# Memory-augmented recurrent attention, forward and backward: the segment chain carries 8 memory tokens instead of 40 tokens

## The chip, the cores and the metric

One core of one Trainium2 chip runs the whole program. The metric is the device time of one execution in microseconds (us), the median of several runs. The profile is one further execution under the hardware profiler; the times of single instructions come from it.

## The reference

Two attention layers over the same 2,048 tokens of 576 features are mixed by a gate, and all gradients are asked for besides the output. Layer A is multi-query attention with 32 heads of 18 (one shared key and value head). Layer B is the recurrent one, and the change touches it alone:

```python
# H = 32 heads of Dh = 128, M = 8 memory tokens, seg_len = 32, n_seg = 64
mask = (idx[:, None] < M) | (idx[:, None] >= idx[None, :])
mem = mem0
for s in range(n_seg):
    xs = x[:, s * seg_len:(s + 1) * seg_len, :].copy()
    h = jnp.concatenate([mem, xs], axis=1)
    q = jnp.einsum('btd,dhe->bhte', h, Wq)      # k and v alike
    scores = jnp.einsum('bhqe,bhke->bhqk', q, k) * scale
    p = _softmax(jnp.where(mask[None, None], scores, -1000000000.0), axis=-1)
    o = jnp.einsum('bhqk,bhke->bhqe', p, v)
    o = jnp.einsum('bhte,hed->btd', o, Wo)
    mem = o[:, :M, :].copy()
    outs.append(o[:, M:, :])
out = g * a + (1 - g) * concatenate(outs)       # g = sigmoid(sum(x * gate_w))
```

Only the 8 memory rows of a segment's output go into the next segment. They are queries over the 32 tokens and the 8 old memory tokens. The 32 token rows are queries too, but what they give is read by nobody within the loop. The kernel returns the output and the gradients of x, of A's four weights, of mem0, of Wq, Wk, Wv, Wo and of the gate's weights.

## The kernel before, in words

Matrices are bf16, sums fp32 in PSUM. A framework takes the program of each engine from the Python loops, allocates tiles from pools with a number of buffers each (`bufs`), sets all semaphores, and orders every engine's instructions ahead of time; an instruction may stand earlier than the loops have it where its operands and buffers allow (the weights of layer B are loaded during pass 2 of layer A). On the chip each engine then works through its list in order. DMAs are issued by SyncE (SP) and GpSimd (POOL), each in its own order too.

`build_full` (L1096) runs these stages one after the other, each with pools of its own:

- **Part A** (`prep`, `a_weights`, `a_setup`, `a_pass1`, `a_pass2`, `a_out`, L717 to L1006): layer A's attention. It also stores x and the weighted gradient of the output, transposed, in DRAM (`xT_dram`, `dbT_dram`). Its pass 2 contains groups of four matmuls on four column strips of TensorE (L984).
- **Forward chain** (`b_forward`, L219): a loop over the 64 segments. `hTs` holds the segment's 32 tokens and 8 memory tokens, transposed and padded to 64 columns. For each of q, k, v, 200 matmuls (L252) make the [64 tokens x 4,096] product in two column halves, with 102 or 103 moving columns each (`pieces`), four banks being evicted by VectorE and ScalarE in turn (`evac`, L88). The 32 heads are transposed on TensorE (L268), scored with the mask added by a second matmul (L282, L284), exponentiated (L287), summed by a matmul with ones (L291), and inverted as a 64x512 reciprocal, four times (L293). Two products give the attention output transposed (L304) and by token (`km_to_tm2`, L307), and 192 matmuls of 8 columns with `WoN` (L314, L317) give the next memory, which L321 to L326 copy into the next `hTs`. q, k, v, the probabilities and outputs of every segment go to DRAM (`st_*`, `ox_dram`, `om_dram`).
- **Weight transposes** (`make_transposed_weights`, L190): all four weights, 640 transposes, through two PSUM buffers, to `st_WT` and `st_WoT`.
- **Combine** (`combine_pass`, L639): per 128 tokens the output product with `WoN` on four column strips (L665), the gate's mix, the output and the gate's gradient.
- **Backward chain** (`b_backward`, L398): the transposed weights are loaded, then the 64 segments run from the last to the first: the output gradient of 40 tokens through `WoT` (L425), score gradients (L448 to L453), the gradients of q, k, v both transposed (L469, L481, L501) and by token (`km_to_tm2`), and 480 matmuls of 40 columns (L515) that give the gradient of the segment's input. Its 8 memory rows are the start of the earlier segment (`gTs`, L523), its 32 token rows go to `dxB_dram`.
- **Weight gradients** (`b_epilogue`, L539): per 512 columns, 20 tiles of 128 tokens (16 of x, 4 of memory) against the gradients of q, k, v (2,400 matmuls), then per 128 columns the same for Wo (1,280 matmuls), with loads of 128x128 pieces (L626).
- **Part A's end** (`a_final`, L1024).

Of the kernel before, what the change touches and what calls it, by code (L numbers as in the profile page):

```python
# [6 lines left out]
ACT = mybir.ActivationFunctionType  # L7
# [13 lines left out]
LP = 64  # L21
# [8 lines left out]

MNK_LIMIT = 960000
BIG_LIMIT = None


def plane(h):
    return h // 16


def ucol(h):
    return (h % 16) // 4, (h % 4) * 128  # L40


def pieces(N, M, K, limit="default"):
    lim = MNK_LIMIT if limit == "default" else limit
    if lim is None or M * N * K <= lim:
        return [(0, N)]
    maxn = max(1, lim // (M * K))
    n = (N + maxn - 1) // maxn
    base = N // n
    rem = N % n  # L50
    out = []
    lo = 0
    for i in range(n):
        sz = base + (1 if i < rem else 0)
        out.append((lo, lo + sz))
        lo += sz
    return out


def pieces_b(N, M, K):  # L60
    return pieces(N, M, K, limit=BIG_LIMIT)


class Kern:
# [41 lines left out]
    def setup_consts(self, pool):  # L106
# [7 lines left out]
        self.onesB = pool.tile([P, 64], BF16, name="onesB")  # L114
        nc.gpsimd.memset(self.onesB[:], 1.0)
        self.negonesB = pool.tile([P, 64], BF16, name="negonesB")
        nc.gpsimd.memset(self.negonesB[:], -1.0)
        mb = pool.tile([P, 64], BF16, name="maskbias")
        nc.gpsimd.memset(mb[:], 0.0)
        nc.gpsimd.affine_select(out=mb[0:64], in_=mb[0:64], compare_op=ALU.is_ge, fill=NEGB,  # L120
                                base=0, pattern=[[1, 64]], channel_multiplier=-1)
        nc.gpsimd.affine_select(out=mb[0:64], in_=mb[0:64], compare_op=ALU.is_ge, fill=0.0,
                                base=31, pattern=[[0, 64]], channel_multiplier=-1)
        nc.gpsimd.affine_select(out=mb[0:64], in_=mb[0:64], compare_op=ALU.is_ge, fill=NEGB,
                                base=39, pattern=[[0, 64]], channel_multiplier=-1)
        nc.gpsimd.affine_select(out=mb[0:32], in_=mb[0:32], compare_op=ALU.is_ge, fill=NEGB,
                                base=39, pattern=[[-1, 64]], channel_multiplier=0)
        nc.gpsimd.affine_select(out=mb[32:64], in_=mb[32:64], compare_op=ALU.is_ge, fill=0.0,
                                base=39, pattern=[[-1, 64]], channel_multiplier=0)
        nc.gpsimd.affine_select(out=mb[32:40], in_=mb[32:40], compare_op=ALU.is_ge, fill=NEGB,  # L130
                                base=39, pattern=[[-1, 64]], channel_multiplier=0)
        self.maskbias = mb

    def setup_dram(self, dram):
        T, NSEG, NM = self.T, self.NSEG, self.NM
        NMP = ((NM + P - 1) // P) * P
        self.xT_dram = dram.tile([NKT, P, T], BF16, name="xT_dram")
        self.st_q2 = dram.tile([NSEG, P, 2048], BF16, name="st_q2")
        self.st_k2 = dram.tile([NSEG, P, 2048], BF16, name="st_k2")
        self.st_vT = dram.tile([NSEG, P, 2048], BF16, name="st_vT")  # L140
        self.st_pnT = dram.tile([NSEG, P, 2048], BF16, name="st_pnT")
        self.st_oT = dram.tile([NSEG, P, 2048], BF16, name="st_oT")
        self.st_WT = dram.tile([3, HB, P, D], BF16, name="st_WT")
        self.st_WoT = dram.tile([NKT, P, J], BF16, name="st_WoT")
        self.ox_dram = dram.tile([T, J], BF16, name="ox_dram")
        self.om_dram = dram.tile([NMP, J], BF16, name="om_dram")
# [1068 lines left out]
```

## Time and profile before

| | us |
|---|---|
| three runs | 13,498.41, 13,510.95, 13,515.17 |
| median | 13,510.95 |
| the profiled execution | 13,530.5 |
| its span, first to last instruction | 13,528.8 |
| PE (TensorE matmul) busy | 11,751.1 (87%) |
| VectorE (DVE) busy | 5,404.0 (40%) |
| ScalarE (ACT) busy | 4,011.9 (30%) |
| GpSimd (POOL) busy | 1,399.6 (10%) |
| mean granted TensorE clock | 0.655 of full speed |
| DMA | 788.49 MB, mean 58 GB/s |

In the lines of the profile L252 and its like appear as L99 and L104: these are the helpers `mm` and `tr` that issue every matmul and transpose, so groups are told apart by their tiles (`pbank<-Wv,hTs` is the projection of v into the PSUM tile `pbank`). "PEld" is the loading of weights into TensorE, which overlaps with matmuls. A group's line gives busy time, then the mean duration of one in ns, then the idle time of the engine before it and what ended it. A timeline's line gives start, duration from the first start to the last end, and, after x, how many instructions were merged. Durations of matmuls overlap, so their rate is read from the starts.

### The profile page before, as it was taken

How to read it: one execution, taken by the hardware profiler on the slowest of the kernel's cores; microseconds unless marked ns; L12 is line 12 of the kernel's file. 1: busy time of each engine (PE TensorE's matmuls, PEld its weight loads, DVE VectorE, ACT ScalarE, POOL GpSimd, SP SyncE). 2: the span in 40 equal slices, each digit the busy share in tenths (PEclk: the TensorE clock that was granted, in tenths of full speed). 3: DMA queues.
4: the chain of work that ended last, by engine and by line, in shares of the span. 5: the costliest groups of instructions: out<-in, count | busy, mean ns of one | idle time of the engine just before them, and what ended most of it. 6: DMA issues, size and time to landing. Idle time of an engine off the chain costs nothing. (4 is left out here: it accounts for less than half of the span.)

```text
span 13528.8 us, 358100 instructions
## 1 busy us (share of the span) xinstructions
PE 11751.1 (87%) x163974; PEld 7294.4 (54%) x163974; DVE 5404.0 (40%) x5901; ACT 4011.9 (30%) x7182; POOL 1399.6 (10%) x2859
## 2 busy tenths in 40 slices
PE   6777777999999999998999999975999999999887
PEld 2222221111266666666666666654878887787333
DVE  5666667888633333333333333321333333333000
ACT  4666666777511111111111111110222222222000
POOL 1111111000000000000000000011111101100235
PEclk9888886555555555555555555556777777767998
DMA  1000003111111111111111111134222222222434
GB/s 56 9 9 9 9 9 96 48 48 48 62 40 37 39 38 38 38 38 37 41 37 39 37 39 37 39 131 144 79 79 82 80 77 79 79 74 76 145 119 110
DMA packets 438733, 788.49 MB, mean 58 GB/s; under 512 B 190529, under 2 KB 279314, under 8 KB 434338
## 3 DMA queue, kind: packets, MB, share of 16 engines
q1 hardware_dynamic: 328930, 458.23, 10.7%
q0 software_dynamic: 108288, 307.35, 6.9%
q8 instruction: 1281, 20.99, 0.6%
q14 instruction: 234, 1.92, 0.0%
HBM read 431.16 MB, written 334.17 MB: 57 GB/s over the span
## 5 line engine op out<-in xcount | busy, mean ns | idle before, releaser
L99 PEld LDWEIGHTS <-hTs 128*64 128x64 bf16 (+1 forms) x38400 | 1854.6, 150 | 886.9 <-ACT hTs L322 25.7
L892 DVE TENSOR_TENSOR a_W<-a_dP,a_E 128x1024 bf16<-128x1024 f32 x1024 | 1251.5, 1224 | 572.8 <-ACT a_E L891 480.3
L979 DVE TENSOR_TENSOR b_dS<-b_dP,b_E 128x1024 bf16<-128x1024 f32 x1024 | 1235.6, 1223 | 204.6 <-PE b_S L99 153.9
L891 ACT ACTIVATE a_E<-a_S 128x512 bf16<-128x512 f32 x2048 | 1115.9, 596 | 447.2 <-PE a_S L99 388.1
L978 ACT ACTIVATE b_E<-b_S 128x512 bf16<-128x512 f32 x2048 | 1110.9, 595 | 349.1 <-DVE b_dS L979 183.2
L293 DVE RECIPROCAL rden<-pbank 64x512 f32<-64x512 f32 x256 | 849.3, 3338 | 424.8 <-PE pbank L99 420.7
L99 PE MATMUL b_S<-b_KV,b_QD 32*128 32x512 bf16 x2048 | 888.1, 583 | 32.0 <-DMA b_QD<-qd_dram 31.9
L99 PE MATMUL pbank<-Wv,hTs 128*64 128x103 bf16 (+3 forms) x12800 | 912.4, 290 | 0.0
L99 PE MATMUL a_acc<-a_W,a_WK 128*64 128x512 bf16 x2048 | 473.0, 449 | 383.6 <-DVE a_W L892 383.4
L99 PE MATMUL pbank<-Wqk,hTs 64*64 64x102 bf16 (+1 forms) x5120 | 752.7, 290 | 0.0
L99 PE MATMUL pbank<-WoT,gTs 128*64 128x103 bf16 (+3 forms) x12800 | 694.9, 239 | 56.5 <-DMA WoT<-st_WoT 56.2
L99 PE MATMUL pbank<-Wq,hTs 128*64 128x103 bf16 (+1 forms) x10240 | 710.1, 290 | 21.6 <-ACT hTs L322 20.3
L99 PE MATMUL pbank<-Wk,hTs 128*64 128x103 bf16 (+1 forms) x10240 | 711.0, 290 | 0.0
L99 PE MATMUL b_acc<-b_dS,b_SD 128*32 128x512 bf16 x2048 | 619.6, 601 | 12.2 <-DVE b_dS L979 10.2
L99 PEld LDWEIGHTS <-gTs 128*64 128x64 bf16 (+1 forms) x12800 | 488.9, 120 | 257.1 <-issue 57.1
L99 PE MATMUL b_acc<-b_E,b_SD 128*32 128x512 bf16 x2048 | 620.3, 602 | 3.1 <-DMA b_SD<-sd_dram 2.1
L99 PE MATMUL b_dP<-b_KV,b_QD 32*128 32x512 bf16 x2048 | 615.1, 597 | 0.0
L99 PE MATMUL a_S<-a_QD,a_KV 32*128 32x512 bf16 x2048 | 539.4, 441 | 45.6 <-ACT a_QD L866 43.1
L99 PEld LDWEIGHTS <-a_WK 128*64 128x64 bf16 x2048 | 193.9, 111 | 688.1 <-issue 681.6
L99 PE MATMUL a_acc<-a_E,a_VK 128*64 128x512 bf16 x2048 | 521.3, 443 | 31.2 <-ACT a_E L891 26.9
L99 PE MATMUL pkq<-maskbias,identB 64*64 64x64 bf16 x2048 | 532.5, 260 | 0.0
L99 PE MATMUL pkq<-qT,kT 128*64 128x64 bf16 x2048 | 532.3, 260 | 0.0
(349 smaller groups left out, 16671.6 us busy)
## 6 DMA issues: line engine op xcount, KB each, us to landing
b_SD<-sd_dram SPq DMA_DIRECT2D x64, 512.0 KB
b_QD<-qd_dram SPq DMA_DIRECT2D x64, 512.0 KB
st_q<-q SPq DMA_DIRECT2D x64, 512.0 KB
st_k<-k POOLq DMA_DIRECT2D x64, 512.0 KB, 3.0
st_vT<-vT SPq DMA_DIRECT2D x64, 512.0 KB
st_pnT<-pnT SPq DMA_DIRECT2D x64, 512.0 KB
st_oT<-oT POOLq DMA_DIRECT2D x64, 512.0 KB, 3.1
bq<-st_q SPq DMA_DIRECT2D x64, 512.0 KB
```

Source lines behind the costliest of these rows:

```text
L99: return self.nc.tensor.matmul(out, lhsT, rhs, start=start, stop=stop, tile_position=tp, skip_group_check=True)
L293: nc.vector.reciprocal(rden[rows, :], den[rows, :])
L891: nc.scalar.activation(Et[:, i, :], S[i][:, :], ACT.Exp, scale=SCALEA)
L892: nc.vector.tensor_tensor(out=Wt[:], in0=dP[:], in1=Et[:], op=ALU.mult)
L978: nc.scalar.activation(Et[:, i, :], S[i][:, :], ACT.Exp, scale=SCALEA)
L979: nc.vector.tensor_tensor(out=dS[:], in0=dP[:], in1=Et[:], op=ALU.mult)
```

## The change

Layer B is written anew; part A and its end are the same code. The stages between them are now:

1. `load_W`, `load_Wo`, then `b_proj_x`: q, k, v of all 2,048 tokens, 128 tokens at a time, with full 128x128 weights and 512 moving columns. Results go to DRAM by token (`xtok`) and transposed (`xTd`).
2. `b_chain_fwd`: the loop over 64 segments with the 8 memory tokens alone (padded to 32 columns). A projection puts four groups of 8 heads on the four column strips of TensorE. The memory queries attend to the segment's 32 tokens, whose keys and values are loaded from DRAM, and to the 8 memory tokens. Keys come by one POOL DMA that picks 32 columns of every head out of `xTd`. The output product is 160 matmuls of 8 columns.
3. `make_transposed_weights`, through four PSUM buffers.
4. `b_bulk`: 16 tiles of 128 tokens, 8 groups of 4 heads: the tokens' attention over the tile's 128 tokens (masked to the own segment) and the 32 memory tokens of its four segments, forward, its score gradients, the gradient of q, the tokens' share in the gradients of the memory's keys and values (`dkx`, `dvx`), the output product, the gate's mix and the gate's gradient. Each group loads 6 tiles and stores 13.
5. `load_WT`, `load_WoT`, then `b_chain_bwd`: the loop from the last segment to the first, memory queries alone. It loads the segment's token keys and values, the memory's q and k, and `dkx`, `dvx`, and ends in 192 matmuls on four strips and an fp32 product that adds the strips.
6. `b_post`: per 128 tokens the gradients of k and v by token (token queries and memory queries) and the gradient of x. Its tiles `sB` and `mB` are filled by 40 DMAs per token tile, with one buffer each.
7. `b_mem_tok`: the memory tokens' gradients and outputs, transposed into token order.
8. `b_dw`: the weight gradients, with one load of all 16 token tiles per 512 columns, for Wo too.

```diff
-        for s in range(NSEG):
-            nc.sync.dma_start(hTs[:, :, 0:SEG], self.xT_dram[:, :, s * SEG:(s + 1) * SEG].rearrange("k p t -> p k t"))
...
-                            for (c, base) in ((u, 0), (u + 4, 64)):
-                                cols = slice(c * 512 + lo, c * 512 + hi)
-                                self.mm(pb[base:base + 64, lo:hi], lhsT=hTs[lrows, kt, :], rhs=wap[rows, cols],
-                                        start=(kt == 0), stop=(kt == NKT - 1), tp=(lrows.start, base))
...
+    def b_proj_x(self, sp, psum):
...
+                    pb = psum.tile([P, 512], F32, name="p_pb", bufs=4)
+                    for kt in range(NKT):
+                        rows = KT_ROWS[kt]
+                        self.mm(pb[:], lhsT=xt[0:rows, kt, :], rhs=self.W[w][0:rows, kt, jc * 512:(jc + 1) * 512],
+                                start=(kt == 0), stop=(kt == NKT - 1))
+                    self.evac(tok[:, jc * 512:(jc + 1) * 512], pb[:])
...
+    def b_chain_fwd(self, keep, sp, psum):
...
+            kx = sp.tile([P, HB, 32], BF16, name="c_kx", bufs=2)
+            nc.gpsimd.dma_start(kx[:], self.xTd["k"][tt][:, :, 32 * sl:32 * sl + 32])
...
+            for w in ("k", "q", "v"):
+                t2 = sp.tile([P, 8, E], BF16, name=f"c_{w}2", bufs=2)
+                for j in range(2):
+                    pj = psum.tile([P, 512], F32, name="c_pj", bufs=3)
+                    for kt in range(NKT):
+                        rows = KT_ROWS[kt]
+                        for c in range(4):
+                            self.mm(pj[32 * c:32 * c + 32, :], lhsT=h_[0:rows, kt, :],
+                                    rhs=self.W[w][0:rows, kt, c * 1024 + j * 512:c * 1024 + (j + 1) * 512],
+                                    start=(kt == 0), stop=(kt == NKT - 1), tp=(0, 32 * c))
...
+            nc.vector.reciprocal(rd[:], den[:])
...
+                    for h in range(HB):
+                        self.mm(pm[0:ncols, kt, :], lhsT=self.WoN[:, h, kt * P:kt * P + ncols],
+                                rhs=oT[:, h % 8, h // 8, :], start=(h == 0), stop=(h == HB - 1))
+                hn = hm[(s + 1) % 2]
+                nc.vector.tensor_copy(hn[:, 0:4, 0:8], pm[:, 0:4, :])
+                nc.scalar.copy(hn[0:64, 4, 0:8], pm[0:64, 4, :])
...
+    def b_bulk(self, keep, wp, sp, psum):
...
+                Sp = psum.tile([P, 4, 256], F32, name="x_big", bufs=2)
...
+                nc.gpsimd.tensor_tensor(out=Pn[:], in0=Et[:], in1=r[:].unsqueeze(2).to_broadcast([P, 4, 160]), op=ALU.mult)
...
+                PT = transp(Pn, "x_PT")
+                po = psum.tile([P, 512], F32, name="x_po", bufs=2)
...
+                nc.gpsimd.tensor_tensor(out=prod[:], in0=dOT[:], in1=oT_g, op=ALU.mult)
+                dP = psum.tile([P, 4, 256], F32, name="x_big", bufs=2)
...
+                for i, h in enumerate(hs):
+                    r32 = slice(32 * i, 32 * i + 32)
+                    nc.sync.dma_start(self.mtok["dkx"][tt * 32:(tt + 1) * 32, h * E:(h + 1) * E], dm_g[r32, 0:128])
+                    nc.sync.dma_start(self.mtok["dvx"][tt * 32:(tt + 1) * 32, h * E:(h + 1) * E], dm_g[r32, 128:256])
...
+    def b_chain_bwd(self, keep, sp, psum):
...
+            nc.gpsimd.dma_start(vxT[:], self.xTd["v"][tt][:, :, 32 * sl:32 * sl + 32])
...
+            ph = psum.tile([P, 1024], F32, name="r_ph", bufs=1)
+            for (lo, hi) in ((0, 512), (512, D)):
+                for wi in (2, 0, 1):
+                    for u in range(8):
+                        for g in range(4):
+                            self.mm(ph[32 * g:32 * g + 32, lo:hi], lhsT=dT[:, wi, u, :], rhs=self.WT[wi][:, 8 * g + u, lo:hi],
+                                    start=(wi == 2 and u == 0), stop=(wi == 1 and u == 7), tp=(0, 32 * g))
...
+    def b_post(self, keep, sp, psum):
...
+            for w in ("q", "dO"):
+                self.load_blockdiag(mB[w], self.mtok[w], tt)
+            for i in range(4):
+                for sl in range(4):
+                    for w, src in (("p", self.pmq_dram), ("ds", self.dsmq_dram)):
+                        nc.sync.dma_start(sB[w][32 * i + 8 * sl:32 * i + 8 * sl + 8, :, 32 * sl:32 * sl + 32],
+                                          src[4 * tt + sl].rearrange("q (g i) k -> q g i k", i=4)[:, :, i, :])
...
+    def b_dw(self, sp, psum):
...
+                t = sp.tile([P, n, 512], BF16, name="w_d", bufs=2)
+                nc.sync.dma_start(t[:, 0:NTT, :], self.xtok[which][:, cs].rearrange("(n p) d -> p n d", p=P))
...
```

More of the change, by code (lines that the diff above doesn't have):

```diff
@@ L20 @@
 SEG = 32
-LP = 64
 NEGB = -30000.0
@@ L29 @@
 KT_ROWS = [128, 128, 128, 128, 64]
[L31 to L61, printed above, removed]
 class Kern:
@@ L210, in make_transposed_weights @@
             for hg in range(8):
[L211 removed]
+                ptr = psum.tile([P, 640], BF16, name="w_ptr", bufs=4)
                 for hl in range(4):
                     h = hg * 4 + hl
[L214 to L215 removed]
+                    self.tr(ptr[0:ncols, hl * E:(hl + 1) * E], self.WoN[:, h, kt * P:kt * P + ncols], P)
```

1093 lines of the change are left out of this document (566 added, 527 removed).

## The prediction

> **What bounds the kernel now.** First the table of busy time by stage, then the timeline inside one segment. Its columns: stretch, its length, busy time (x instructions) of PE, weight load, VectorE (DVE), ScalarE (ACT), GpSimd (POOL), granted TensorE clock, DMA share, GB/s.
>
> ```profile
> span 13528.8 us, 358100 instructions
> ```
>
> ```profile
> 0.00:3648.00 3648.00, 2986.12 (x18241) 764.72 (x18242) 2563.32 (x2272) 2443.24 (x4497) 360.42 (x934) 0.72 0.11 35
> 3648.00:8901.00 5253.00, 4758.03 (x66107) 3437.53 (x66106) 1648.62 (x1662) 744.18 (x1280) 264.37 (x384) 0.50 0.11 39
> 8901.00:9003.00 102.00, 90.40 (x649) 63.29 (x653) 30.63 (x70) 42.30 (x68) 28.08 (x52) 0.50 0.58 210
> 9003.00:9342.00 339.00, 186.04 (x8222) 167.07 (x8213) 39.53 (x105) 10.17 (x16) 24.62 (x48) 0.74 0.38 130
> 9342.00:9398.00 56.00, 0.64 (x2) 0.10 (x3) 5.08 (x8) 0.04 (x1) 26.71 (x50) 0.51 0.95 323
> 9398.00:12523.00 3125.00, 2898.48 (x66368) 2504.65 (x66368) 1041.19 (x1664) 711.86 (x1216) 319.24 (x706) 0.75 0.27 78
> 12523.00:13134.00 611.00, 549.83 (x2399) 237.25 (x2400) 40.69 (x59) 35.02 (x60) 161.34 (x304) 0.98 0.42 136
> 13134.00:13398.00 264.00, 193.57 (x1283) 74.29 (x1281) 12.48 (x17) 10.21 (x16) 170.76 (x324) 0.95 0.39 95
> 13398.00:13529.00 131.00, 87.95 (x718) 45.53 (x718) 22.50 (x45) 14.88 (x29) 44.08 (x58) 0.83 0.40 130
> ```
>
> The rows are part A (3,648 us), forward chain (5,253), weight transposes (102), combine (339), weight reload (56), backward chain (3,125), weight gradients (611 and 264) and part A's end (131). Part A and its end, 3,779 us, stay; 9,750 us are rewritten. A segment costs 5,253/64 = 82.1 us forward and 3,125/64 = 48.8 us backward. PE is busy for over 90% of both, so PE work and what its order waits for bound them.
>
> ```profile
> 6220.09 14.26 PE L99 MATMUL pbank<-Wv,hTs 128*64 128x103 bf16 x200
> 6234.28 1.67 PE L104 MATMUL ptrh<-identB,q 64*128 64x64 bf16 x32
> 6246.70 6.76 DVE L293 RECIPROCAL rden<-pbank 64x512 f32<-64x512 f32 x2 [5.81 <-PE pbank L99]
> 6266.20 6.63 PE L99 MATMUL psmall<-oT,WoN 128*128 128x8 bf16 x182
> 6272.92 0.19 ACT L321 CAST hTs<-psmall 128x32 bf16<-128x32 f32 x1 [6.75 <-PE psmall L99]
> 6273.16 0.56 PE L99 MATMUL pbank<-Wq,hTs 128*64 128x103 bf16 x8 [0.33 <-ACT hTs L322]
> ```
>
> Here 200 matmuls project one of q, k, v in 14.3 us, so 43 of 82 us are projections of 40 tokens, 32 of which depend on no memory. Four reciprocals take 13.5 us. The part that is truly recurrent at the end, the output product into 8 columns, takes 6.6 us (36 ns each), and the next projection starts 0.33 us behind it. The change leaves 8 tokens in this loop.
>
> **The forward chain afterwards.** Its projections use four column strips with 512 moving columns. The nearest row is pass 2 of part A, also at half clock:
>
> ```profile
> 3000.97 0.61 PE L99 MATMUL b_acc<-b_dS,b_SD 128*32 128x512 bf16 x2
> 3000.98 0.61 PE L99 MATMUL b_acc<-b_E,b_SD 128*32 128x512 bf16 x2
> 3001.52 0.61 PE L99 MATMUL b_dP<-b_KV,b_QD 32*128 32x512 bf16 x2
> ```
>
> Four strips start within 0.01 us and the next four 0.54 us later: they run at once. The weight-gradient stage takes 611/2,400 = 0.2546 us per 512-column matmul at clock 0.98, doubled 0.51; I take 0.50 per group of four. Per segment:
>
> - 3 x 10 groups: 15.0 us (against 42.8); 24 transposes of 128 columns, by the 32 of 64 columns in 1.67 us: 2.6;
> - 64 score matmuls and a mask at 36 ns: 2.4;
> - softmax on 128x64 instead of four reciprocals of 512: exponent 0.5, sums 0.4, reciprocal 64/512 of 3.38 = 0.5, scaling 0.3, expansion 0.7;
> - 16 products 0.8, copy 0.6, 160 output matmuls at 36 ns 5.8, copy and hop 0.5.
>
> Sum 30.1, taken as 30: 64 x 30 = 1,920 us. Loads of the next segment are double-buffered, behind 30 us of work; about 18 SyncE issues fit:
>
> ```profile
> 11032.06 0.30 SPq L377 DMA_DIRECT2D dkx_dram<-dX  x1
> 11054.21 0.38 SPq L405 DMA_DIRECT2D gTs<-dbT_dram  x1
> L94 DVE CAST dX<-pbank 128x512 bf16<-128x512 f32 x384 | 258.3, 686 | 469.1 <-DMA dqm_dram<-dX 374.1 <-PE pbank L99 95.0
> L96 ACT CAST dX<-pbank 128x512 bf16<-128x512 f32 x384 | 212.7, 590 | 568.4 <-DMA dqm_dram<-dX 495.0 <-PE pbank L99 71.8 <-ACT dKT L96 0.4
> L96 ACT COPY qT<-ptrh 128x1024 bf16<-128x1024 bf16 x64 | 64.8, 1012 | 24.0 <-PE ptrh L104 24.0
> L294 DVE TENSOR_TENSOR pnT<-pexp,rden 64x512 bf16<-64x512 bf16 x256 | 165.0, 683 | 3.9
> L949 POOL TENSOR_TENSOR a_SD<-a_qt,a_rl 128x512 bf16<-128x512 bf16 x64 | 66.8, 1044 | 0.0
> L519 DVE CAST dhT<-pdh 128x160 bf16<-128x160 f32 x64 | 20.8, 324 | 354.0 <-PE pdh L99 354.0
> ```
>
> 18 x 0.36 = 6.5 us. **The backward chain**: dO 10 groups 5.0, last eviction and hop 0.9, transposes and copy 1.2, 64 + 8 score matmuls 2.5, dS with its 32x32 transposes and expansions 2.3, products 1.4, copy 0.5, the 192 strip matmuls into dh 9.5 (24 groups of 512 and 24 of 64 columns are 14, of which the dV third can start before dS), eviction 0.6, fp32 sum over strips 1.2, copies 0.4: 25.5 us, 1,630 us. The fp32 sum, the 32x32 transposes on DVE and the broadcast expansions don't occur before; by the smallest and the largest small operation in these rows each lies between 0.2 and 1.1 us, which for the eight of them on the path is 5 us a segment either way; I take values near 0.5, since all but the fp32 sum work on 256 or 512 columns. Its 36 SyncE DMAs take 36 x 0.36 = 13 us, under cover as long as a segment is longer.
>
> **The bulk stages.** Bulk projection: 48 x (40 matmuls x 0.2546 + 32 transposes x 0.08) = 612 us; per step DVE evicts 4 x 0.69 + 2 x 0.69 = 4.1 us and ACT 4 x 0.59 + 2 x 1.01 = 4.4, hidden under 12.8. If PE stays at half clock it is 1,100. Weight transposes get four PSUM buffers for two: 75 (floor 640 x 0.104 = 67 by the transposes above). Attention over 128-token tiles: a group of four heads streams 9,728 columns, 4.8 us at 0.2546/512 per column, 9.7 at half clock; DVE 3.4, ACT 2.9, POOL 3.9 with two 1.0 to 1.3 us multiplications, SyncE 16 issues 5.8. The dependent path through one group is about 14 us and the PSUM pairs let two be in flight: 8 us a group, between 5.8 and 11. 128 x 8 + 16 output products at 10 = 1,184; combine (339) is inside it. Reload of weights as before: 60, and 25 ahead of the bulk. Later token gradients: 10,496 columns per group, 5.2 us; per tile 40 SyncE loads into single-buffered tiles, 14.4 us, most of it bare: 16 x (8 x 5.2 + 13) = 874. Memory-token transposes: 4 x (4.2 MB at 323 GB/s 13 + two POOL copies of 4,096 elements 16.7 + 6) = 144. Weight gradients: the same matmuls; the 128-column pieces of the output weight's loads become 512-column ones, so 264 falls to its PE time, 205; with a 15 us start 831.
>
> **Sum**: 3,779 + 15 (first loads) + 612 + 1,920 + 75 + 25 + 1,184 + 60 + 1,630 + 874 + 144 + 831 = 11,149 us of span, against 13,528.8. The profiled execution took 13,530.5 us, 1.7 around its span; the median of the three runs is 13,510.95, 20 lower. So 11,130.
>
> The Trainium skill, TensorEngine Tiling (Array Packing), Instruction Overhead, says that each matmul carries about 60 cycles, so that one moving column costs as much as 60. At 1.2 GHz that would be an estimated 50 ns where 182 matmuls of 8 columns took 36 ns each; over about 390 small matmuls in a pair of segments the sum would be some 350 us higher. The measurement decides.
>
> **Rivals.**
>
> *The chains run faster (chance 0.20).* The combine stage, also four column strips, was granted 0.74 and the backward chain 0.75. At 0.75 the streamed parts (15.0 and 14.5 us) lose a third: (5.0 + 4.8) x 64 = 630, so 10,500. Against it: the forward chain stayed at 0.50 although PE was busy 91%. The Trainium skill, TensorE: Matmul & The Clock Gate, Part 1, says that about 3.4 us of sustained activity releases the full clock; by that rule this rival wins. The forward row disagrees, the combine row half agrees.
>
> *The engines' orders cost more than the dependent path (0.19).* Every engine takes its instructions in order; a store that waits on SyncE holds the loads behind it, and a reader of those waits on PE. Segments of 38 and 34 us and groups of 11 us add 512 + 544 + 384: 12,570. Against it: the 0.33 us hop in the forward chain. For it: there the longest waits of the other engines are whole stretches of a segment, for PE or for a copy, as in this answer on waits (total, times, longest).
>
> ```profile
> ACT dX L96 <- DMA dqm_dram<-dX: 495.0, 64, 8.9
> ACT gTs L523 <- DVE dhT L520: 462.5, 64, 8.6
> ```
>
> *Slower: the chains become bound by loads in 64-byte runs (0.05).* Each segment fetches keys or values of 32 tokens out of a transposed array on POOL's queue, 4,096 runs.
>
> ```profile
> L227 POOL DMA_DIRECT2D mThist<-in_B_mem_dram x5: 692/880/937, 2166.3 to 2185.4; - x5
> DMA to landing us min/median/max: 19.1/30.8/37.8
> 2160.00:2212.00 52.00, 32.46 (x277) 9.83 (x277) 38.95 (x35) 38.04 (x71) 11.24 (x13) 0.83 1.02 311
> q1 hardware_dynamic: 328930, 458.23, 10.7%
> ```
>
> Loads of 1,024 runs landed after 30.8 us; four times that, two in flight, is a load every 62 us: 128 x (62 - 27.75) more, about 15,500. It decides from 27.75 + 2,380/128 = 46 us per load. Against it: those loads stood in a stretch with DMA share 1.02, and the mean packet of queue 1 takes 10.7% x 16 x 13,528.8 / 328,930 = 70 ns, so 4,096 on 16 engines take at most 18 us.
>
> That the chain isn't shortened at all (13,511) I give 0.01: the diff shows the 40-token products gone from the loop.
>
> **Numbers.** The forecast, 0.55, holds 10,550 to 12,000 from the bounds of the group (5.8 to 11 us) and of the strips (0.46 to 0.55 us). With the faster rival and the longer orders the range is 10,250 to 12,600. 0.2% (27 us) is about what a measurement of this kernel can tell from no change: faster 0.94, same 0.01, slower 0.05.
>
> **What would show it.** In the changed profile: a forward segment of 30 us with projections of about 5 us per weight and 160 output matmuls in 5.8; a backward one of 25.5 with a product into dh of 10 to 14; bulk projection 612; groups of 8 us; gaps of about 13 us per tile in the token gradients; weight gradients 831. Segments over 46 us with PE waiting on DMA, or a bulk above 2,500 us, would make it wrong.

## The result, and the profile after

The changed kernel takes 11,412.64 us, the median of four runs (11,406.79 to 11,418.36), beside 13,504.68 us for the kernel before in the same job (four runs, 13,494.86 to 13,515.17). The ratio is 0.845, with a 95% interval of 0.844 to 0.847. The forecast was 11,130 us, 2.5% low. Its sum came out near for a poor reason: two large errors of opposite sign stand in it.

The table of busy time by stage of the changed kernel, a stage running from its first matmul to that of the next. The columns are those of the first table of the prediction: stretch, length, PE, weight load, VectorE, ScalarE, GpSimd, granted clock, DMA share, GB/s.

```profile
span 11405.0 us, 219104 instructions
```

```profile
0.00:3660.00 3660.00, 3015.23 (x18232) 771.84 (x18240) 2557.56 (x2272) 2443.77 (x4497) 359.55 (x970) 0.71 0.11 35
3660.00:4252.00 592.00, 581.48 (x3396) 241.85 (x3461) 199.23 (x288) 209.66 (x288) 2.21 (x3) 1.00 0.45 181
4252.00:5719.00 1467.00, 1258.14 (x24628) 693.36 (x24624) 291.31 (x642) 166.39 (x387) 132.55 (x190) 0.75 0.25 45
5719.00:5810.00 91.00, 82.09 (x641) 56.08 (x642) 30.35 (x69) 41.65 (x69) 20.31 (x12) 0.56 0.65 227
5810.00:7781.00 1971.00, 1322.25 (x9744) 725.06 (x9888) 502.05 (x1024) 360.96 (x656) 516.89 (x646) 0.60 0.42 116
7781.00:9376.00 1595.00, 1155.50 (x23751) 603.19 (x23752) 304.62 (x900) 116.36 (x320) 197.37 (x354) 0.64 0.30 65
9376.00:10453.00 1077.00, 644.13 (x5776) 376.46 (x5886) 151.29 (x384) 160.26 (x272) 166.48 (x313) 0.80 0.42 121
10453.00:10590.00 137.00, 42.01 (x533) 38.13 (x535) 30.92 (x44) 33.27 (x36) 37.41 (x15) 0.65 0.86 319
10590.00:11273.00 683.00, 678.44 (x3610) 318.50 (x3678) 53.38 (x76) 45.32 (x76) 64.14 (x106) 1.00 0.44 146
```

| stage | forecast, us | measured, us | difference |
|---|---|---|---|
| part A, its end (the last 132 us), first loads | 3,794 | 3,792 | -2 |
| bulk projection | 612 | 592 | -20 |
| forward chain | 1,920 | 1,467 | -453 |
| weight transposes | 75 | 91 | +16 |
| bulk attention and its lead-in | 1,209 | 1,971 | +762 |
| reload and backward chain | 1,690 | 1,595 | -95 |
| token gradients | 874 | 1,077 | +203 |
| memory-token transposes | 144 | 137 | -7 |
| weight gradients | 831 | 683 | -148 |

Two rows say most of it. The forward chain was granted 0.75 of the clock, not 0.50. And in the bulk stage PE is busy 1,322 of 1,971 us, with VectorE, ScalarE and GpSimd busy for less than a third each: none of the four is at its limit, so something waits in turn.

The inside of one forward segment, TensorE's timeline (start, duration of the merged group, count, and in brackets the idle time before it):

```profile
5003.28 0.18 PE L66 MATMUL c_sm<-c_PB,c_vx 128*128 128x32 bf16 x1 [1.58 <-DVE c_PB L201]
...
5004.39 5.35 PE L66 MATMUL c_pm<-c_oT,WoN 128*128 128x8 bf16 x160 [0.42 <-DVE c_oT L282]
5010.09 4.30 PE L66 MATMUL c_pj<-Wk,hm 128*32 128x512 bf16 x40 [0.35 <-DVE hm L295]
...
5015.73 2.24 PE L66 MATMUL c_pj<-Wq,hm 128*32 128x512 bf16 x31
...
5022.29 0.40 PE L71 MATMUL c_pt<-identB,c_v 128*128 128x128 bf16 x4 [0.17 <-ACT c_v L63]
...
5023.58 0.22 PE L66 MATMUL c_sm<-c_E,blockones 128*128 128x64 bf16 x2 [0.50 <-ACT c_E L265]
```

The projection of k takes 4.30 us here for its 40 matmuls, that is 0.43 per group of four, and 31 of q's 40 take only 2.24, about 0.29. The same work runs at two clocks within one segment. In this segment the clock rises near the end of k's projection; 41 of the 63 that follow the first segment run wholly at half clock and take 4.81 us, 0.48 per group, which is the median too. The output product is 160 matmuls in 5.35 us. TensorE waits for the softmax 0.50 and 1.58 us.

### The profile page after: what moved, and what is told of

Its sections match the earlier page's. It is cut to its first block, busy times and chain, and to the rows that moved or that the text cites. A ratio compares the mean times of both kernels' runs of the same rounds, so it can differ in the third digit from the quotient of the medians.

```text
span 11405.0 us, 219104 instructions
## 1 busy us (share of the span) xinstructions
PE 8865.9 (78%) x91009; PEld 3869.9 (34%) x91416; DVE 4143.1 (36%) x5742; ACT 3592.5 (31%) x6629; POOL 1540.5 (14%) x2664
## 5 line engine op out<-in xcount | busy, mean ns | idle before, releaser
L66 PE MATMUL r_ph<-WT,r_dT 128*32 128x512 bf16 x12288 | 562.0, 353 | 29.5 <-ACT r_dT L608 29.5
L66 PE MATMUL w_acc<-w_d,w_h 128*128 128x512 bf16 (+1 forms) x2352 | 523.1, 380 | 37.5 <-DMA w_d<-dqx_dram 34.8
L679 DVE COPY y_T<-y_pt 128x512 bf16<-128x512 bf16 x384 | 151.3, 422 | 934.8 <-PE y_pt L71 920.5
L66 PE MATMUL a_dP<-a_QD,a_KV 32*128 32x512 bf16 x2048 | 455.6, 441 | 0.0
L66 PE MATMUL y_pdx<-WT,y_T 128*128 128x64 bf16 (+1 forms) x2976 | 426.5, 289 | 24.1 <-ACT y_dx L685 10.9
L66 PE MATMUL c_pm<-c_oT,WoN 128*128 128x8 bf16 (+1 forms) x10080 | 340.3, 173 | 38.4 <-DVE c_oT L282 27.0
L66 PEld LDWEIGHTS <-r_dT 128*32 128x32 bf16 x12288 | 256.4, 109 | 334.9 <-issue 217.6
L66 PEld LDWEIGHTS <-b_SD 128*32 128x32 bf16 x4096 | 120.6, 101 | 731.1 <-issue 725.5
L66 PEld LDWEIGHTS <-WoN 128*128 128x128 bf16 (+1 forms) x10080 | 338.1, 114 | 50.9 <-issue 49.6
L66 PE MATMUL y_pk<-y_qB,y_dsB 128*128 128x512 bf16 x112 | 49.9, 446 | 391.9 <-DMA y_dsB<-dsmq_dram 391.9
```

The source lines that it names most:

```text
L66: return self.nc.tensor.matmul(out, lhsT, rhs, start=start, stop=stop, tile_position=tp, skip_group_check=True)
L679: nc.vector.tensor_copy(tT[:], pt[:])
```

## The experiments

Each is an edit of the changed kernel. The kernels e1 to e10 were timed once each. Stages are therefore compared by their length in the profiles: the forward chain takes 1,461 to 1,467 us in the seven kernels that leave it alone, while part A, which no edit touches, varies from 3,636 to 3,680. The single times of whole kernels are given beside; differences of some 40 us between them say nothing.

### Bulk attention: which of queue and dependent path

Within a tile of the changed kernel a score gradient starts every 13.23 us (the median of the starts; here two on the timeline, each with the exponent of the next group, `x_E`, behind it):

```profile
6849.76 0.82 DVE L446 SCALAR_TENSOR_TENSOR x_dS<-x_big,x_P 128x640 bf16<-128x640 f32 x1 [2.56 <-PE x_big L66]
6850.05 0.70 ACT L391 ACTIVATE x_E<-x_big 128x640 bf16<-128x640 f32 x1 [3.98 <-PE x_big L66]
...
6863.00 0.82 DVE L446 SCALAR_TENSOR_TENSOR x_dS<-x_big,x_P 128x640 bf16<-128x640 f32 x1 [2.56 <-PE x_big L66]
6863.30 0.70 ACT L391 ACTIVATE x_E<-x_big 128x640 bf16<-128x640 f32 x1 [3.98 <-PE x_big L66]
```

The exponent of a group is followed by that group's score gradient 13.0 us later, and the exponent of the group after it starts only then: the groups follow one another.

Eight of them are 106 us of the 1,971/16 = 123 that a token tile takes; from the last group of a tile to the first of the next it is 31.3 us (median). SyncE's 16 issues per group or the path through the engines could set the 13.23.

**Fewer stores (e1_merge).**

```diff
-                for i, h in enumerate(hs):
...
-                    nc.sync.dma_start(self.mtok["dkx"][tt * 32:(tt + 1) * 32, h * E:(h + 1) * E], dm_g[r32, 0:128])
-                    nc.sync.dma_start(self.mtok["dvx"][tt * 32:(tt + 1) * 32, h * E:(h + 1) * E], dm_g[r32, 128:256])
+                nc.sync.dma_start(self.dmx_dram[tt, g], dm_g[:])
```

> The eight small stores per group of the bulk stage (the token share in the gradients of the memory's keys and values) become one store of 128x256 into an array of its own, and the backward chain reads that array in 256-byte runs. Theory (the group is one dependent path through PE, ScalarE, VectorE and GpSimd, 13.2 us from one group's score gradient to the next): the bulk stage stays at 1,971 us within 40. Rival (SyncE's ordered queue of 16 issues sets the group): seven issues of 0.42 us fewer are 2.9 us per group, 128 x 2.9 = 376 us, so the bulk stage takes about 1,600.

Measured: bulk stage 1,924 us, 47 less; the kernel 11,363.4. The path's forecast was a change within 40, missed by 7, the queue's 376 less. The groups still follow at 13.24 us; the gain is all at the change of tiles, 27.8 us instead of 31.3. The queue does not set the group.

**Three groups in flight (e2_pipe).** The same instructions and queues in another order of the program, with one buffer more where a tile now lives longer, and the loads of a tile's own operands ahead of its start:

```diff
+        for k in range(NI + 2):
...
+            if mid:
+                f_PT(mid)
+            if back:
+                f_dP(back)
+            if mid:
+                f_o(mid)
+            if front:
+                f_scores(front)
+            if back:
+                f_DT(back)
...
```

> The same instructions of the bulk stage, written so that three groups of heads are in flight: scores and output gradient of group k, attention output of group k-1, score gradients of group k-2, alternating on TensorE; loads of a token tile go out four groups ahead. Same queues, same loads and stores, four buffers instead of three for the loaded tiles. Theory (dependent path): PE is left with its own work, 1,322 us busy at a clock of 0.60, so the bulk stage falls to 1,400 or below; if PE is then busy over 95% of a stretch the clock rises and it may reach 1,100. Rival (SyncE's ordered queue): the same 16 issues in the same queue, the stage stays above 1,850.

The stage's row in the table of busy time:

```profile
5814.00:7231.00 1417.00, 989.03 (x9743) 581.45 (x9888) 510.90 (x1025) 357.33 (x656) 518.87 (x642) 0.85 0.59 160
```

Measured: 1,417 us instead of 1,971, 17 above the expected 1,400; the kernel 10,851.0. Groups follow at 10.29 us (the median; by their place in the tile 5.9 to 12.2), and 20.1 at the change of tiles, where the early loads of the next tile have their part. In the changed kernel PE waited for loads at the changes of tiles only, so what shortened the groups within a tile is the order, and the clock that rose with it. SyncE issues as much as before, so the dependent path was the bound. The row shows a second gain: PE's busy time fell from 1,322 to 989 us with the same instructions, because the clock went from 0.60 to 0.85. A denser PE became a faster PE. SyncE is near its limit now: in this kernel its 16 issues of one group fill 8.9 of the 10.3 us (6500.32 to 6509.20):

```profile
6500.32 0.34 SPq L384 DMA_DIRECT2D x_qT<-qxT_dram  x1
...
6504.40 1.44 SPq L502 DMA_DIRECT2D dkxm_dram<-x_dm  x1
6505.89 0.41 SPq L503 DMA_DIRECT2D dvxm_dram<-x_dm  x1
...
6509.20 0.37 SPq L384 DMA_DIRECT2D x_qT<-qxT_dram  x1
```

PE's largest wait is for another engine, GpSimd's multiplication into `x_P` (total, times, longest):

```profile
PE x_tr L71 <- POOL x_P L423: 193.2, 106, 2.2
```

### Token gradients: loads into single buffers

TensorE's largest wait in that stage of the changed kernel (total, times, longest):

```profile
PE y_pk L66 <- DMA y_dsB<-dsmq_dram: 391.9, 16, 25.4
```

The 16 small loads of this kind per tile, with as many of `y_pB` (min, median, max of the issue in ns):

```profile
L650 SPq DMA_DIRECT2D y_dsB<-dsmq_dram x254: 651/651/679, 9375.4 to 10406.9; - x127
```

**Two buffers (e3_post).**

```diff
-        mB = {w: keep.tile([P, 8, 4, E], BF16, name=f"y_{w}B") for w in ("q", "dO")}
+        mBs = [{w: keep.tile([P, 8, 4, E], BF16, name=f"y_{w}B{i}") for w in ("q", "dO")} for i in range(2)]
...
+            mB, sB = mBs[tt % 2], sBs[tt % 2]
```

> In the token-gradient stage the tiles that hold the block-diagonal memory operands (40 loads per token tile) get two buffers instead of one. Theory (the 32 loads of 0.65 us and 8 more stand bare ahead of each tile because the buffer is free only when the tile before is done): PE's waits for them, 392 + 100 us in 16 tiles, mostly go, and the stage falls from 1,088 to about 700, PE's busy 644 and a little. Rival (the issues themselves are the bound: 40 loads and about 37 other issues on SyncE are some 39 us per tile, and a load still waits behind stores in the queue): the stage stays above 950.

Measured: 867 us, 210 less; the kernel 11,176.3. Both expectations missed, and the answer lies between. The wait for `y_dsB` falls from 391.9 to 136.7 us, but does not go:

```profile
PE y_pk L66 <- DMA y_dsB<-dsmq_dram: 136.7, 13, 11.6
```

In this kernel's SyncE timeline a small load follows the other every 0.69 to 0.70 us, so 32 of them take 22 of the 867/16 = 54 us of a tile, and the loads of the next groups stand behind them:

```profile
9840.85 0.65 SPq L652 DMA_DIRECT2D y_pB<-pmq_dram  x1
9841.55 0.65 SPq L652 DMA_DIRECT2D y_dsB<-dsmq_dram  x1
```

The buffer was one half of the cost, the issues the other. The combined kernel below, with half of these loads issued by GpSimd, has 651 us in this stage, at PE busy 622.

### Backward chain: a copy behind a load on GpSimd's queue

**Padding copies on ScalarE (e6_padact).** In the changed kernel GpSimd issues the load of transposed values (`r_vxT`) for a later segment ahead of the padding copies of this one:

```profile
8609.62 1.68 POOL L521 DMA_DIRECT2D r_vxT<-vxT_dram  x1 [19.34 <-PE r_sm L66]
8611.29 0.25 POOL L539 COPY r_ppad<-r_pT 128x64 bf16<-128x64 bf16 x1
...
8612.57 0.19 PE L66 MATMUL r_pkv<-r_PqB,r_dOm 128*128 128x32 bf16 x1 [2.96 <-DVE r_PqB L201]
```

The copy's operand `r_pT` has long been there. But the load waits 19.34 us for its buffer, takes 1.68 to issue, and only then comes the copy for which TensorE idles 2.96 us.

```diff
-                nc.gpsimd.tensor_copy(pad[:, :, 0:8], u8(src))
+                if nm in ("p", "px"):
+                    nc.scalar.copy(pad[:, :, 0:8], u8(src))
+                else:
+                    nc.gpsimd.tensor_copy(pad[:, :, 0:8], u8(src))
```

> In the backward chain the two padding copies of the stored probabilities are done by ScalarE instead of GpSimd; everything else is the same. Theory (on GpSimd these copies stand behind the load of transposed values for a later segment, which waits for its buffer and then takes 1.7 us to issue, so TensorE waits 3.0 us per segment for the expanded probabilities): the wait goes, 64 x 2 to 3 us, and the stage falls from 1,595 us to 1,400 to 1,470. Rival (the score gradients are late anyway; another wait of the same length takes its place): it stays above 1,550.

```profile
7780.00:9168.00 1388.00, 1088.69 (x23751) 577.83 (x23752) 298.62 (x899) 134.96 (x448) 158.81 (x225) 0.74 0.34 74
```

Measured: 1,388 us, 207 less, or 3.2 per segment, a little more than expected; the kernel 11,195.4. PE's waits for the expanded probabilities fall from 181.1 us to 1.9, so the queue theory holds. With these waits gone the granted clock is 0.74 instead of 0.64, and PE's busy time falls from 1,155.5 to 1,088.7 us, which is part of the gain.

### Forward chain: the strips

**Inner loops exchanged (e5_loop).**

```diff
-                    for kt in range(NKT):
-                        rows = KT_ROWS[kt]
-                        for c in range(4):
+                    for c in range(4):
+                        for kt in range(NKT):
+                            rows = KT_ROWS[kt]
```

> In the projections of the forward chain the two inner loops change places: all five pieces of one column strip are issued before the next strip's, so that neighbouring matmuls are of the same strip. Same matmuls, same results. Theory (four strips run at once, and that is what shortened a projection from 14.3 to 2.9 to 4.3 us): 120 matmuls of 512 columns run one after the other, 0.213 us each at full clock and 0.427 at half, 25.6 to 51 us per segment for now about 10, and the stage grows from 1,463 us by 1,000 to 2,600. Rival (the saving comes from having fewer columns and tokens, strips gain nothing): the stage stays within 50 us.

```profile
6035.96 11.80 PE L66 MATMUL c_pj<-Wk,hm 128*32 128x512 bf16 x40 [0.35 <-DVE hm L295]
```

Measured: the stage takes 2,896 us, 1,429 more; the kernel 12,859.4. The same 40 matmuls take 11.80 us (a median of 12.2) instead of 4.81, though the clock of the stage is higher, 0.88. Of the 3,786 us by which the stage became shorter, the order of issue, neighbours on different strips, is worth 1,429; the other 2,357 remain without it. Set against the gain of the whole kernel it is two thirds (1,429 of 2,092 us), since the tokens' work, taken out of the loop, costs time in stages of its own.

### Forward chain: what grants the clock

**Ballast (e4_ballast).** Matmuls without a reader, to keep TensorE busy during the softmax:

```diff
+            bal = psum.tile([P, 512], F32, name="c_pj", bufs=3)
+            for i in range(16):
+                self.mm(bal[:, 0:128], lhsT=self.identB[:], rhs=self.W["k"][:, 0, 0:128])
             rd = sp.tile([P, 64], F32, name="c_rd", bufs=2)
```

> In the forward chain 16 matmuls of 128 columns with no reader are added to each segment, in the stretch in which PE waits for the softmax (1.6 us); results are unchanged. Theory (the clock goes by whether PE was busy in the stretch of about 3.4 us before: full after more than 95% busy, kept while over 80%): the clock of the chain rises from 0.75 to above 0.9, the projection of k falls from 4.3 to about 2.2 us and a segment from 22.9 to about 20: 64 x 2.9 = 190 us less in that stage, 1,280 instead of 1,463. Rival (the clock falls with the share of time that PE works, as in the old forward chain, which was 91% busy at 0.50): the clock goes down towards 0.5, and the segment takes 25.5 or more, 1,630.

Measured: stage 1,463 us, clock 0.79; the kernel 11,388.8. The projection of k still took 4.8 us. Neither expectation held: the clock rose a little, and nothing was won, since kernels without this edit have 1,461 to 1,467 too.

**More ballast (e7_ballast2).** The same matmuls at three places:

```diff
+            self.ballast(psum, 10)
             den = psum.tile([P, 64], F32, name="c_sm", bufs=2)
...
+            self.ballast(psum, 30)
             rd = sp.tile([P, 64], F32, name="c_rd", bufs=2)
...
+            self.ballast(psum, 8)
             oT = sp.tile([P, 8, 4, 8], BF16, name="c_oT", bufs=2)
```

> The ballast again, sized by what the first one showed (PE was still idle 1.0, 0.5 and 0.2 us in the stretch of the softmax, so the stretch was only 55% to 65% busy and the clock fell behind it): 10, 30 and 8 matmuls of 128 columns without a reader, behind the scores, behind the sums and behind the products. Theory (full clock is kept while PE is busy over about 80% of the last 3.4 us): the clock of the forward chain goes above 0.95, the projection of k falls from 4.3 to 2.2 us, and the stage from 1,463 us to 1,280 to 1,330. Rival (the clock has a budget, a stretch at full clock is paid for by a later one at half): the clock stays at 0.75 to 0.8 and the stage at 1,460 or above.

Measured: stage 1,441 us, clock 0.85; the kernel 11,394.9. Again neither expectation held. The table of busy time in steps of 2 us shows where the clock was lost (the last three numbers of a row are the clock, the DMA share and GB/s):

```profile
5002.00:5004.00 2.00, 2.00 (x87) 2.00 (x84) 0.00 (x0) 0.00 (x0) 0.00 (x0) 1.00 0.91 100
...
5008.00:5010.00 2.00, 2.00 (x24) 0.43 (x20) 0.00 (x0) 0.05 (x1) 0.00 (x0) 0.50 0.00 0
```

In the first, PE is busy the whole 2 us, with 87 matmuls of 8 columns of the output product, and behind it, in the projection of k, the clock is at half. So "busy" is not what counts. The next guess was the number of columns that stream. They are counted from the traces: the clock changes only in steps of 3.41 us, and for each such stretch the table gives the moving columns per ns (a matmul is taken to stream from its start, at 2.4 columns per ns at full clock and 1.2 at half, and overlapping ones count once; the weight-gradient stage, 2,400 matmuls of 512 columns and 640 pairs of 512 and 64 in 683 us, has 2.34 at clock 1.00) and the clock of the stretch that follows. It joins the forward chains of the changed kernel, of e7 and of the two runs below, and the bulk stages of the changed kernel and of e2.

| columns per ns | from half: next full / next half | from full: next full / next half |
|---|---|---|
| below 0.8 | 12 / 642 | 0 / 351 |
| 0.8 to 1.0 | 141 / 68 | 38 / 36 |
| 1.0 and more | 232 / 1 | 1,106 / 0 |

In these six stages one bound, about 0.9 columns per ns, fits both directions. It also fits the old forward chain: its projection moved 200 x 103 columns in 14.26 us, which is 1.44 per ns and more than half clock can stream, so the matmuls ran in pairs: 0.72 per ns. Of its stretches 1,432 lie below 0.8 and 106 between 0.8 and 1.0, and none was followed by full clock, though PE was busy 91% of the time. The projection of k in the new chain moves 10 groups of 512 columns in 4.81 us at half clock, 1.06 per ns, and full clock follows.

It is not a rule for every stage. In the old backward chain both outcomes occur between 0.8 and 1.2: of 165 stretches at half clock with 1.0 and more, 116 were followed by half. And pass 2 of part A contradicts it: in the trace of the changed kernel 319 of its 429 stretches have 1.0 to 1.06, and the clock stayed at half throughout, with PE busy 1,430 of 1,467 us. The median of the stretches after which the new forward chain's clock rose is 1.06, their lowest 0.94. What else enters is open.

**Ballast and a wide output product (e9_wide).** Here 24 columns of zeros are added to the 8 of the output product, so that it streams more without computing more.

```diff
+        oWs = [sp.tile([P, 8, 4, 32], BF16, name=f"c_oW{i}", bufs=1) for i in range(2)]
...
+            nc.vector.tensor_copy(oW[:, :, :, 0:8], po[:].rearrange("p u (c q) -> p u c q", q=8))
...
-                                rhs=oT[:, h % 8, h // 8, :], start=(h == 0), stop=(h == HB - 1))
+                                rhs=oW[:, h % 8, h // 8, :], start=(h == 0), stop=(h == HB - 1))
```

> The ballast of 10, 30 and 8 matmuls, and the 160 matmuls of the output product move 32 columns instead of 8, 24 of them zeros that nobody reads (the attention output is copied into a zeroed tile for it; a second copy is stored). Results are unchanged. Theory (the clock of a stretch of 3.4 us goes by how many columns streamed in the stretch before: in the traces it rises from half above roughly 0.8 of the half rate and is kept above roughly 0.4 of the full rate, about 0.95 columns per ns both times; 8 columns per 27 ns are 0.3): 32 columns per 27 to 33 ns are 1.0 to 1.2, so the clock of the chain goes above 0.95, the projection of k falls from 4.3 to about 2.2 us, the product stays at 4.3 to 5.5 us, and the stage falls from 1,441 us with ballast alone to 1,270 to 1,330. Rival (a budget: full clock for at most 17 us, then half): the clock stays at about 0.85 and the stage at 1,440 or above.

```profile
4228.00:5564.00 1336.00, 1267.29 (x27705) 785.66 (x27705) 292.60 (x645) 190.13 (x451) 132.46 (x190) 0.96 0.27 50
```

```profile
5008.31 2.67 PE L66 MATMUL c_pj<-Wk,hm 128*32 128x512 bf16 x40 [0.35 <-DVE hm L307]
```

Measured: clock 0.96, stage 1,336 us; the kernel 11,261.0. The clock goes where the bound puts it, and a stretch at full clock lasts up to 198 us here, which the budget of the rival does not allow. The stage misses the expected 1,330 by 6 us: the projection of k takes 2.67 us, not 2.2, and in 29 of the output products PE stands for about 1 us with no wait that the profile shows.

**The wide product alone (e10_wideonly).** The edit of e9 without the three calls of `ballast`.

> The wide output product of the forward chain alone, without the ballast. Theory (columns streamed in the 3.4 us before set the clock, rising above about 0.95 columns per ns): the softmax still drops the clock to half, and 160 matmuls of 32 columns at 33 ns each, 0.97 columns per ns, stand about at the bound, so that the clock is often full again when the projection of k begins: the stage takes 1,340 to 1,420 us, clock 0.8 to 0.9. Rival (with the ballast it was the share of time in which TensorE works that mattered, not the width): as before, 1,463 within 20, clock 0.75.

```profile
4242.00:5596.00 1354.00, 1144.33 (x24632) 655.82 (x24632) 292.24 (x646) 190.28 (x451) 132.55 (x190) 0.83 0.26 49
```

Measured: 1,354 us at clock 0.83, as the theory has it; the kernel 11,291.3. PE's busy share is no higher than in the changed kernel (1,144 of 1,354 and 1,258 of 1,467), yet the clock rises. Moving four times the columns at nearly the same issue rate saved 113 us.

### Weight gradients: the width of Wo's loads

**Pieces of 128 columns again (e8_dwpieces).**

```diff
-                nc.sync.dma_start(t[:, 0:NTT, :], self.xtok[which][:, cs].rearrange("(n p) d -> p n d", p=P))
...
+                step = 128 if which == "o" else 512
+                for lo in range(0, 512, step):
...
+                    nc.sync.dma_start(t[:, 0:NTT, lo:lo + step], self.xtok[which][:, c1].rearrange("(n p) d -> p n d", p=P))
```

> In the weight gradients the tokens' attention output for Wo is loaded in pieces of 128 columns again, as in the kernel before, four loads of 16 token tiles for one. Theory (the old stage for Wo, 264 us, had its 60 us above the PE time of such matmuls from these loads): the stage grows from 683 us to about 740. Rival (two buffers and 20 us of matmuls per 512 columns cover the pieces too, and the new stage is shorter because the loads of a whole 512-column block are issued early, not because of their width): 683 within 10.

Measured: 682 us; the kernel 11,393.3. The rival's number holds: the width is not what the stage gained by. Which part of the new stage's loading (whole blocks, two buffers, both inputs kept in SBUF) removed the old stage's waits was not tried.

### Together

**The parts that won (f1_all)**, with the bulk's normalized probabilities on VectorE as a further edit:

```diff
-                nc.gpsimd.tensor_tensor(out=Pn[:], in0=Et[:], in1=r[:].unsqueeze(2).to_broadcast([P, 4, 160]), op=ALU.mult)
+            nc.vector.tensor_tensor(out=Pn[:], in0=Et[:], in1=r[:].unsqueeze(2).to_broadcast([P, 4, 160]), op=ALU.mult)
```

> Together: the bulk stage with three groups in flight, its eight small stores merged to one, and the normalized probabilities made on VectorE instead of GpSimd; in the backward chain the two padding copies on ScalarE; in the token gradients two buffers for the memory operands, with half of the 32 small loads issued by GpSimd. Theory (the stages end where TensorE's own work and its order set them, and the parts add up): the bulk stage 1,417 less 50 to 250, the backward chain 1,388, the token gradients below 867, at most 780: 11,405 less 600 to 800, less 207, less 300, about 10,150 us. Rival (POOL and SyncE queues were not what kept the last two stages): bulk 1,400 and token gradients 860, about 10,440.

Bulk, backward chain and token gradients of this kernel:

```profile
5817.00:6884.00 1067.00, 873.65 (x9889) 519.64 (x9889) 610.01 (x1154) 356.56 (x657) 355.62 (x515) 0.94 0.77 213
6884.00:8290.00 1406.00, 1088.97 (x23749) 579.25 (x23748) 298.11 (x898) 134.79 (x448) 177.94 (x246) 0.73 0.34 75
8290.00:8941.00 651.00, 622.29 (x5888) 365.00 (x5888) 151.78 (x384) 155.66 (x272) 308.57 (x557) 0.98 0.72 200
```

Measured: 9,886.3 us, a ratio to the kernel before of 0.730 (0.726 to 0.734), about 260 better than expected. In the bulk stage the merged stores and the move to VectorE took 350 us more; groups follow at 6.37 us, at a clock of 0.94. Which of the two it was is open. In the kernel with three groups in flight the filled SyncE speaks for the stores, which were worth little while the path was the bound, and PE's largest wait, 193.2 us for `x_P` from GpSimd, speaks for the move.

**With the forward chain's edits (f2_all).** The kernel above with the edits of e7 and e9.

> The combined kernel of 9,886 us with the ballast and the wide output product in the forward chain. Theory (the forward chain's own time falls by 127 us and nothing else is touched): 9,886 - 127, about 9,760. Rival (the two don't add, since heat or a budget takes back the clock in the other stages): 9,850 or above.

Measured: 9,760.7 us, a ratio of 0.723 (0.721 to 0.725). The forward chain takes 1,328 us in it, and the other stages are those of the kernel above, as the first expectation has it.

## Why the prediction was right, and where it was wrong

**The main step held.** The loop carries 8 tokens, its projections run on four strips at once (e5 undoes that: 1,429 us), and the 160 small matmuls take 5.35 us for a forecast 5.8. Part A, the bulk projection, the transposes of memory tokens and the sum of the backward chain are within 6% of their terms. The weight transposes took 91 us for 75, PE being busy 82 of them at a clock of 0.56.

**Forward chain: 30 us a segment forecast, 22.9 measured.** The step that failed is "I take 0.50 per group of four", not as a price but as a price for all 30 groups of a segment. At half clock a group costs 0.48 (4.81/10), so the price was right; at full it costs 0.27 (2.67/10 in e9), and the projections of q and v mostly ran there, as the two clocks of the segment above show. From the projection of k to the last transposes of v it is 12.6 us (5010.09 to 5022.69 in the timeline) for 17.6 forecast. From the first scores to the output product it is 4.6 us for 6.2, and 0.9 of it runs beside v's transposes.

The rival "the chains run faster", at 0.20, was right on the forward chain's clock, 0.75; the backward chain, where it had 0.75 too, was granted 0.64. The reason held against it failed: that the old chain stayed at 0.50 while busy 91% is no evidence on a chain whose projections stream 1.06 columns per ns at half clock instead of 0.72. The Trainium skill, TensorE: Matmul & The Clock Gate, Part 1, which that rival cited, has a busy window of about 3.4 us release the full clock. The runs agree on the length of the window (steps of 3.41 us). In the six stages counted, what made it busy was columns streamed, not matmuls in flight; pass 2 of part A shows that this is not all.

**Bulk attention: 8 us a group forecast, 13.2 measured, and 17 per tile besides for 10.** The step that failed is "the PSUM pairs let two be in flight: 8 us a group". The path of about 14 us was near: 13.0 us lie between a group's exponent and its score gradient. But buffers only allow overlap; the order of TensorE's program has to contain it, and there a group's score gradient is followed by its own transposes and products, with the next group's scores alone drawn ahead. e2 puts three groups into that order and gets 1,417 us. The rival on the engines' orders had the direction with 11 us a group, and named the wrong place there: stores on SyncE hold loads, but e1 shows that those eight stores cost 47 us. In the backward chain its mechanism was at work, on GpSimd's queue (e6).

**Token gradients: 13 us bare per tile forecast, 392/16 = 24.5 in PE's largest wait.** The step priced 40 loads at 0.36 us; the 32 small ones take 0.65 each. The mechanism was right; the price was read from a store and a load of other shapes (0.30 and 0.38). The length of the runs does not explain it: that load, `gTs`, has 640 runs of 64 bytes, and these have 64. Why they take longer is open.

**Backward chain: right in the sum, not in its parts.** TensorE's timeline of one segment has dO at 3.74 us for 5.0 forecast, and the whole product into dh at 8.82 for 14, of which 9.5 were counted on the path:

```profile
8603.17 3.74 PE L66 MATMUL r_pj<-WoT,dm 128*32 128x512 bf16 x40 [0.28 <-DVE dm L627]
...
8616.05 8.82 PE L66 MATMUL r_ph<-WT,r_dT 128*32 128x512 bf16 x192 [0.46 <-ACT r_dT L608]
```

The step "of which the dV third can start before dS" did not happen: all 192 matmuls stand behind the copy `r_dT`, and that starts at 8615.62, behind the last product with the score gradient (8615.40). The shorter products hid this, and a wait of about 3 us that the sum does not have: a copy behind a load on GpSimd's queue (e6).

**Weight gradients: 831 forecast, 683 measured.** The duration of 0.2546 us per matmul was the length of the old stage divided by its matmuls, waits included. PE was busy 550 of those 611 us. The new stage has few waits (busy 678 of 683).

**The slower rival** needed 46 us per load of 64-byte runs. Such a load lands after 6.6 us:

```profile
L221 POOL DMA_DIRECT2D c_kx<-kxT_dram x64: 1680/1681/1697, 4258.2 to 5666.8; - x64
...
DMA to landing us min/median/max: 5.9/6.6/7.4
```

Its bound of 18 us was the better guide than the old loads in a stretch with busy DMA engines, but by luck: it was read from the packets of queue 1, and these loads are on GpSimd's own queue 0, where the trace counts 5,120 packets for all 64 of them.

## What to carry to other kernels

When a stage is forecast from a dependent path and a number of buffers, look in the engine's program order for the overlap: without it the path is the price, and here writing it in, with earlier loads, was worth 554 us. A busy share says little on the clock; count the columns that stream as well, and try whether a product with few columns can be made wider: here it cost nothing. A duration taken from a stage must be the engine's, not the stage's length divided by a count, and an issue's price belongs to its shape.

## What the runs showed of the hardware

- The granted clock moved between half and full in steps of 3.41 us, and in the six stages counted it followed the columns streamed in the stretch before: below 0.8 per ns half (993 of 1,005), from 1.0 on full (1,338 of 1,339). In pass 2 of part A 319 stretches with 1.0 to 1.06 were all followed by half, and the old backward chain shows both outcomes: the count of columns alone does not decide.
- 160 matmuls of 8 columns take 5.35 us at half clock, 33 ns each, and 4.45 us at full, 28 ns each (12 of the 13 segments of the kernel with more ballast whose output product ran wholly at full clock). Matmuls of 32 columns run at the same rate at full clock (160 in 4.47 us in the last kernel). In some segments PE stops inside the product with no wait that the profile shows, as after 130 matmuls for 0.70 us in the kernel with more ballast.
- The issue of a DMA on SyncE took 0.37 us for a 128x512 store and 0.65 for a load of 64 runs of 64 bytes, though in the kernel before a load of 640 such runs (`gTs`) took 0.38; on GpSimd a load of 4,096 such runs took 1.68.
- The same multiplication of 128x640 took 0.83 us on VectorE and 1.25 on GpSimd.
